# One written-out order for the middle stage of the first sequence, some of its units filtered on GpSimd, and the imaginary filter pieces loaded first

## The chip, the cores and the metric

The kernel runs on one core of a Trainium2 chip. Its time is the device time of one execution in microseconds. Three runs of the kernel before gave 859.03, 859.19 and 859.25 us, a median of 859.19 us. The five engines of the core have one instruction queue each, worked strictly in the order written: TensorE (PE; its weight loads are shown as PEld), VectorE (DVE), ScalarE (ACT), GpSimd (POOL) and SyncE (SP, which here only issues DMAs). An engine at whose head an instruction waits for a semaphore does nothing else meanwhile.

## The reference

The kernel computes a spectral filter along the sequence followed by a normalized gated feed-forward block. It takes x (8 sequences, 3008 positions, 256 channels), a complex filter per frequency and channel (1505 x 256, real and imaginary parts apart), and the weights of the block.

```python
X = np.fft.rfft(x, axis=1)
Y = X * (filt_r + 1j * filt_i)[None, :, :]
x = np.fft.irfft(Y, n=3008, axis=1).reshape(24064, 256)
xn = x / np.sqrt(np.mean(x * x, axis=-1, keepdims=True) + 1e-06) * rms_g
g = xn @ w_gate                                   # 256 -> 1536
out = (g / (1 + np.exp(-g)) * (xn @ w_val)) @ w_out   # 1536 -> 256
```

All matrix products run on fp16 operands with fp32 sums; inputs and output are float32.

## The kernel before

**The transform.** 3008 is 47 x 64. A sequence goes through four matrix stages. Stage A (`a0_unit`, `a_unit`) is a real transform over 64 points, a product with the 128 x 128 table `wa`. Stage B (`b_unit`) is, for each of K2 = 32 values k2, a complex transform over 47 points with twiddle factors, a product of a 96-row tile with the 96 x 96 table `wb[:, k2]`. Then comes the filter. The inverse of B (`bi_unit`, table `wi`) writes the buffer `uu`, and the inverse of A (`n_unit`, table `wai`) gives the filtered sequence. `wb` and `wi` have 128 rows; only the first 96 (KR) enter a product.

**Units.** Stage B, the filter and the inverse of B work in 16 units per sequence, called u = 2 g + dh: g is a group of four k2 and dh one half of the 256 channels. For a unit, four matmuls fill a PSUM tile of 128 x 384 (`psb`). The complex multiplication is two elementwise products, the halves of `s_part`: e = 0 multiplies by the real filter (columns 96 to 143 of `ff`), e = 1 multiplies the tile with real and imaginary parts exchanged by minus the imaginary filter and the imaginary filter (columns 0 to 95 of `ff`). Each half is one VectorE instruction of 128 x 384 (lines 238 and 241).

**Sequence 0 and the others.** Sequence 0 goes ahead of everything and is kept on the chip: between A and B it is turned by TensorE (`tr0_unit`, eight units of four k2, copied from PSUM to the tiles `t2`), and behind the filter `yt0_unit` adds the two halves and turns them in one go, by eight matmuls with the identity into a PSUM tile `psy`, copied to `yt`. Then `bi_unit` follows and its copy into `uu`. The stage from `tr0_unit` to the last copy into `uu` is called the middle stage here. Sequences 1 to 7 are spread over the feed-forward work of the sequence before; they go through memory between A and B (`z_store`, `t2_load`), add their halves on GpSimd and turn by a DMA transpose. For sequence 1, units 2, 6, 10 and 14 already go through `b_soft`: ScalarE copies `psb` to SBUF and GpSimd does both halves (GpSimd does not read PSUM in this kernel).

**The filter.** `f_load(i, f)` loads filter rows in three blocks i of 512 rows, f = 0 the imaginary and f = 1 the real part, into three float32 buffers `fs`. `f_unit(i, f, dh)` turns one block and channel half by four TensorE transposes and copies the pieces into `ff`. `f_neg` then fills the negated imaginary columns on GpSimd, and `f_last` a corner.

**The queue of GpSimd** issues most loads: x (`x_load`), the filter, `wb`, `wi`, the gate and value weights (`w_load`, three thirds q into staging buffers) and the down weights (`wo_load`). The DMAs that GpSimd issues take eight landing semaphores in turn, and an issue waits until the DMA that had its semaphore before has landed. `w_gain(q)` scales a third of the gate and value weights by the norm's gain into `wg` and `wv`. A staging buffer comes free for a new load when what was in it has been read; the four of them serve `fs`, `ws` and later the tiles y.

**Behind the middle stage.** `t4_load` turns `uu` by four DMA transposes on SP's queue. `t4_first` and `first_norm` bring the first tile of 512 positions to the feed-forward block without waiting for these. A small copy `seen` (line 681) holds GpSimd's queue until the second of the four transposes has landed. Then the feed-forward block begins: 8 x 6 tiles of 12 steps each (`gv`: two matmuls for the gate, two for the value, SiLU on ScalarE, product on VectorE; `down`: four matmuls). The work of later sequences is laid between these steps by a plan that is made when the kernel is built (`fit`, `at`): each step has room for one more PSUM tile and some time on ScalarE and VectorE. For sequence 1 the plan puts the 12 `a_unit`s (line 204) one to a step from the fifth on; units 6 to 8 read the x chunk that `x_load(1, 2)` brings, units 9 to 11 that of `x_load(1, 3)`.

**The order around the change** is written out by hand in the block under `tc.manual_schedule()`: first the loads, then `fill`s (matmuls without use for their result), stage A of sequence 0, the filter units between the turning units, and a loop over positions p that runs `b_unit`, both halves, `yt0_unit` two positions later and `bi_unit` four positions later. In it VectorE does all 32 halves, ScalarE nearly all copies of `psy` and `psi`; GpSimd issues loads and runs `f_neg` and all three `w_gain`.

Of the kernel before, what the change touches and what calls it, by code (L numbers as in the profile page):

```python
# [10 lines left out]
FP32 = mybir.dt.float32  # L11
FP16 = mybir.dt.float16
# [8 lines left out]
P = 128  # L21
# [80 lines left out]
def kernel(  # L102
# [83 lines left out]
            nc.gpsimd.dma_start(t.rearrange("p a d -> p (a d)"), src(N2, XC))  # L186
        st[b]["x"][c] = t

    def bank(i, name):
        pool, tag = ((psM, "mx"), (psG, "pg"), (psV, "pv"), (psB, "mb"), (psO, "po0"))[i]  # L190
        return pool.tile([P, 512], FP32, tag=tag, name=name)

    def copy(eng, out, in_, scale=None):
        if eng == "A":
            nc.scalar.activation(out=out, in_=in_, func=AXT.Copy, **({} if scale is None else {"scale": scale}))  # L195
        elif scale is None:
            nc.vector.tensor_copy(out=out, in_=in_)
        else:
            nc.vector.tensor_scalar(out=out, in0=in_, scalar1=scale, scalar2=None, op0=ALU.mult)
# [30 lines left out]
    def s_part(b, i, e, eng=None):  # L230
        eng = eng or nc.vector
        g, dh = divmod(i, 2)
        ps, s = st[b]["s"][i]
        fv = ff[:, dh, 4 * g:4 * g + 4, :]
        o = s[e].rearrange("p k (r q) -> p k r q", r=2)
        if e == 0:
            f1 = fv[:, :, 2 * SL:3 * SL].unsqueeze(2).to_broadcast([P, 4, 2, SL])
            eng.tensor_tensor(out=o, in0=ps, in1=f1, op=ALU.mult)  # L238
        else:
            f2 = fv[:, :, 0:2 * SL].rearrange("p k (r q) -> p k r q", r=2)  # L240
            eng.tensor_tensor(out=o, in0=ps[:, :, ::-1, :], in1=f2, op=ALU.mult)  # L241
# [35 lines left out]
    def yt_tile(b, g):  # L277
        st[b]["yt"][g] = ytp.tile([P, 4, 2, P], FP16, tag="yt", name="yt")
# [90 lines left out]
        copy(eng, va[:, dh].rearrange("p k (m i) -> p (k m) i", m=NR)[:, :, 4 * gq:4 * gq + 4],  # L369
             ps.rearrange("p (u t) -> p t u", u=4))  # L370

    def tr0_unit(g, eng):
        pool, tag = ((psO, "po0"), (psO, "po1"), (psM, "mx"))[g % 3]
        ps = pool.tile([KR, 4, 2, P], FP16, tag=tag, name="pst")
        for k in range(4):
            for dh in range(2):
                nc.tensor.transpose(ps[:, k, dh, :], va[:, dh, 4 * g + k, :], ident)  # L377
        c, r = divmod(g, 2)
        if c not in st[0]["t2"]:
            t2_tile(0, c)  # L380
        copy(eng, st[0]["t2"][c][:, 4 * r:4 * r + 4, :].rearrange("p k (e d) -> p k e d", e=2), ps)
# [13 lines left out]
    def f_unit(i, f, dh, e):  # L395
        t = fst[i]
        ps = bank(1 + "AV".index(e), "psf").rearrange("p (a q) -> p a q", a=FR4)
        for a in range(FR4):
            nc.tensor.transpose(ps[:, a, :], t[:, f, a, ds(dh * P, P)], idf)  # L399
        v = ps.rearrange("p a (q s) -> p s a q", s=16)  # L400
        fk = ff[:, dh, 0:K2].rearrange("p (t k) c -> p t k c", k=4)
        fu = ff[:, dh, 1:K2 + 1].rearrange("p (t k) c -> p t k c", k=4)[:, ::-1, ::-1, :]
        lo = SL * (1 + f) + 8 * i
        hi = lo + H
        if i < 2:
            copy(e, fk[:, :, :, lo:lo + 8], v[:, 0:8])
            copy(e, fu[:, :, :, hi:hi + 8], v[:, 8:16])
        else:
            copy(e, fk[:, :, :, lo:lo + 8], v[:, 8:16])
            copy(e, fu[:, :, :, hi:hi + 7], v[:, 0:8, :, 1:8])  # L410
# [6 lines left out]
    def f_neg(k0, n, dhs=(0, 1)):  # L417
        for dh in dhs:
            nc.gpsimd.tensor_scalar(out=ff[:, dh, k0:k0 + n, 0:SL], in0=ff[:, dh, k0:k0 + n, SL:2 * SL],  # L419
                                    scalar1=-1.0, scalar2=1.0, op0=ALU.mult, op1=ALU.mult)  # L420

    def yt0_unit(i, eng, bk, ks=slice(0, 4)):
        g, dh = divmod(i, 2)
        s = st[0]["s"][i][1]
        ps = bank(bk, "psy")[0:KR].rearrange("p (k t) -> p k t", k=4)
        for k in range(4)[ks]:
            for e in range(2):
                nc.tensor.matmul(ps[:, k, :], s[e][:, k, :], ident, start=(e == 0), stop=(e == 1))  # L428
        if g not in st[0]["yt"]:
            yt_tile(0, g)  # L430
        copy(eng, st[0]["yt"][g][0:KR, ks, dh, :], ps[:, ks])

    def fill(n, bk=0):
        ps = bank(bk, "pf")
# [120 lines left out]

    wst = {}

    def w_load(q):
        cols = ts(q, DFF // 3)
        t = stg.tile([P, 2, 2, DFF // 3], FP32, tag="stg", name="ws")  # L560
        for src, k in ((moe_w_gate, 0), (moe_w_val, 1)):
            nc.gpsimd.dma_start(t[:, k], src.rearrange("(dt p) j -> p dt j", p=P)[:, :, cols])
        wst[q] = t

    def wo_load(q):
        nc.gpsimd.dma_start(wo[:, ts(q, JT // 3), :],
                            moe_w_out.rearrange("(jt p) d -> p jt d", p=P)[:, ts(q, JT // 3), :])
# [10 lines left out]
    with tc.manual_schedule():  # L578
# [19 lines left out]
        nc.vector.memset(mhalf, -0.5)  # L598
        nc.vector.memset(ones, 1.0)
        for t in ss3[1:]:  # L600
# [23 lines left out]
        a0(3)  # L624
        fill(4)
        a0(4, 5)
        todo = [(i, f, dh) for i in range(2) for f in range(2) for dh in range(2)][:7] + [(2, 0, 0)]
        for u in todo[0:2]:
            f_unit(*u, "A")
        for g in range(7):  # L630
            tr0_unit(g, "V")
            if g < 6:
                f_unit(*todo[g + 2], "A")
        f_neg(4, 4, (0,))
        f_neg(8, 8, (0,))
        UN = K2 // 2
        od = [2, 4, 6, 3, 5, 7, 0, 1] + list(range(8, UN))
        tr0_unit(7, "V")
        for p in range(2):
            b_unit(0, od[p], (0, 3)[p], 1)  # L640
        f_unit(1, 1, 1, "A")
        f_unit(2, 0, 1, "A")
        b_unit(0, od[2], 4, 1)
        f_unit(2, 1, 0, "A")
        for p in range(3):
            s_part(0, od[p], 0)
        for p in range(UN + 3):
            if 3 <= p < UN:
                b_unit(0, od[p], (0, 3)[p % 2])
                s_part(0, od[p], 1)  # L650
            if p == 0:
                f_unit(2, 1, 1, "A")
                f_neg(4, 12, (1,))
                f_last()
                f_neg(0, 4)
# [10 lines left out]
            if p == UN + 1:  # L666
                yt0_unit(UN - 1, "V", 1, slice(0, 2))
                yt0_unit(UN - 1, "A", 0, slice(2, 4))
            if 4 <= p < UN + 3:
                bi_unit(0, od[p - 4], "AV"[p == UN + 1], 2)  # L670
            if UN + 1 <= p < UN + 3:
                fill(1, 1)
        bi_unit(0, UN - 1, "V", 3, slice(0, 2))
        bi_unit(0, UN - 1, "A", 0, slice(2, 4))
        a_unit(1, 0, "A", 1)
        t4_first()
        a_unit(1, 1, "V", 0)
# [1 line left out]
        for c in range(NXC):  # L679
            t4_load(0, c)  # L680
        nc.gpsimd.tensor_copy(out=seen, in_=st[0]["t4"][1][:, 0, 0:4])
# [188 lines left out]
```

## Time and profile before

| what | value |
|---|---|
| median of 3 runs | 859.19 us (859.03 to 859.25) |
| profiled execution, device time | 859.02 us |
| its span in the profile | 857.2 us |
| busy, TensorE / VectorE / ScalarE / GpSimd | 849.3 / 556.1 / 612.8 / 300.4 us |
| first filter half on VectorE | 21.54 us |
| last copy into `uu` on VectorE ends | 38.91 us |
| first gate matmul | 43.12 us |
| granted TensorE clock | 1.00 |

Times are counted from the start of the span. The profiled execution takes 1.8 us more than its span, for what lies around it. In the order of time a row gives the start, the length from the first to the last instruction of the row, the engine, the line of the kernel, the operation, the tiles (output <- input) with their sizes, how many instructions are merged in the row, and in brackets how long the engine stood idle before it and what ended the wait. In the table by stretches the columns are the stretch and its length, the busy time and count of instructions of TensorE, weight loads, VectorE, ScalarE and GpSimd, the granted clock, the share of time that the 16 DMA engines were busy, and GB/s. A row on DMA issues gives the size of one and the microseconds from issue to landing.

### The profile page before, as it was taken

The page shows a single profiled execution, that of the slowest core. Times are in us where ns is not written, and L with a number is a line of the kernel's source. Part 1 is how long each engine was busy: PE and PEld are TensorE (multiplying, and loading weights), DVE is VectorE, ACT ScalarE, POOL GpSimd, SP SyncE. Part 2 cuts the span into 40 slices and gives each one's busy share as a digit, 9 for nine tenths or more (in the row PEclk, how much of TensorE's full clock was granted, in tenths as well). Part 3 has the DMA queues.
Part 4 walks back from the last instruction along what each step waited for, and adds up shares of the span by engine and source line. Part 5 has one row for each costly group of instructions (what it writes and reads, how often), then busy time and mean ns, then how long its engine had stood idle before and what let it go on. Part 6 is the DMA issues. An engine that isn't in the chain of part 4 may idle for free.

```text
span 857.2 us, 16980 instructions
## 1 busy us (share of the span) xinstructions
PE 849.3 (99%) x6117; PEld 531.9 (62%) x6117; DVE 556.1 (65%) x922; ACT 612.8 (71%) x1343; POOL 300.4 (35%) x349
## 2 busy tenths in 40 slices
PE   8999999999999999999999999999999999999997
PEld 6756666666656666666666666666666666665654
DVE  5857655776666666666666676767666665555554
ACT  4986878786687757887578865887567765777444
POOL 5725732543154413443144430444123430132000
PEclk9999999999999999999999999999999999999999
DMA  9997698756976566747746648534554331521101
GB/s 284 271 182 151 148 191 162 148 124 143 186 137 133 117 134 119 158 113 129 157 126 110 130 99 172 119 77 117 129 115 93 99 72 41 125 52 50 63 25 50
DMA packets 199293, 108.24 MB, mean 126 GB/s; under 512 B 159622, under 2 KB 183576, under 8 KB 199208
## 3 DMA queue, kind: packets, MB, share of 16 engines
q1 hardware_dynamic: 190520, 85.78, 44.2%
q0 software_dynamic: 8544, 21.24, 12.8%
q8 instruction: 48, 0.79, 0.4%
q14 instruction: 37, 0.30, 0.1%
q10 hardware_dynamic: 144, 0.13, 0.0%
HBM read 45.78 MB, written 35.65 MB: 95 GB/s over the span
## 4 chain that ended last, share of the span: by engine, by line
PE 97%; DMA 1%; DVE 0%; ACT 0%; POOL 0%; issue 0%; POOLq 0%
PE po L526 29%; PE pv L501 28%; PE pg L501 28%; PE psb L248 3%; PE psi L292 3%; PE psn L321 2%; PE psa L204 2%; DMA fs<-in_filt_i_dram 1%; PE psy L428 1%; PE psf L399 1%; PE pst L377 0%; POOL xc L186 0%; DVE s L238 0%; ACT ff L195 0%; ACT sq L458 0%
## 5 line engine op out<-in xcount | busy, mean ns | idle before, releaser
L506 DVE TENSOR_TENSOR hh<-pv,sg 128x512 f16<-128x512 f32 (+1 forms) x577 | 391.5, 679 | 284.0 <-ACT sg L505 219.9
L505 ACT ACTIVATE sg<-pg 128x512 f16<-128x512 f32 (+1 forms) x577 | 337.5, 585 | 214.5 <-PE pg L501 210.7
L501 PE MATMUL pg<-xn,wg 128*128 128x512 f16 (+2 forms) x1156 | 337.9, 374 | 0.0
L501 PE MATMUL pv<-xn,wv 128*128 128x512 f16 (+2 forms) x1156 | 337.8, 374 | 0.0
L526 PE MATMUL po<-wo,hh 128*128 128x256 f16 x2256 | 332.6, 272 | 0.0
L526 PEld LDWEIGHTS <-hh 128*128 128x128 f16 x2256 | 213.5, 98 | 105.5
L275 POOL TENSOR_TENSOR ss<-s,s 128x384 f16<-128x384 f16 x112 | 101.9, 911 | 267.1 <-DVE s L241 239.5
L501 PEld LDWEIGHTS <-wv 128*128 128x128 f16 x1156 | 113.0, 98 | 130.6 <-issue 0.2
L501 PEld LDWEIGHTS <-wg 128*128 128x128 f16 x1156 | 111.6, 98 | 16.8 <-issue 0.2
L347 POOL TENSOR_TENSOR xt<-y,rho 128x1024 f16<-128x1024 f32 (+1 forms) x47 | 87.3, 1858 | 2.9
L329 ACT ACTIVATE junk<-y 128x256 f16<-128x256 f32 x184 | 76.0, 413 | 2.9
L241 DVE TENSOR_TENSOR s<-psb,ff 128x384 f16<-128x384 f32 x124 | 67.6, 547 | 0.3 <-POOL ff L419 0.3
L238 DVE TENSOR_TENSOR s<-psb,ff 128x384 f16<-128x384 f32 x124 | 67.6, 547 | 0.3 <-ACT ff L195 0.2
L195 ACT ACTIVATE uu<-psi 128x384 f16<-128x384 f32 (+1 forms) x127 | 61.8, 487 | 1.0
L195 ACT ACTIVATE y<-psn 128x512 f32<-128x512 f32 (+1 forms) x95 | 55.8, 588 | 4.4 <-PE psn L321 0.2
L292 PEld LDWEIGHTS <-yt 96*128 96x128 f16 x512 | 35.5, 97 | 26.2 <-issue 0.2
L339 POOL TENSOR_TENSOR rho<-u,mhalf 128x4 f32<-128x4 f32 (+1 forms) x47 | 47.6, 1012 | 3.9
L337 POOL TENSOR_SCALAR u<-ss 128x4 f32<-128x4 f32 (+1 forms) x47 | 9.1, 194 | 106.4 <-ACT junk L329 105.2
L292 PE MATMUL psi<-wi,yt 96*128 96x96 f16 x512 | 42.9, 205 | 0.0
L195 ACT ACTIVATE t<-psa 128x512 f16<-128x512 f32 x69 | 40.9, 594 | 2.4 <-PE psa L204 0.9
L248 PE MATMUL psb<-wb,t 96*128 96x96 f16 x480 | 40.0, 206 | 0.0
L248 PEld LDWEIGHTS <-t 96*128 96x128 f16 x480 | 29.3, 97 | 10.7 <-issue 0.2
(91 smaller groups left out, 361.0 us busy)
## 6 DMA issues: line engine op xcount, KB each, us to landing
out_dram<-o SPq DMA_DIRECT2D x40, 512.0 KB, 3.6
xc<-in_x_dram POOLq DMA_DIRECT2D x31, 384.0 KB, 5.7
z_tmp<-t SPq DMA_DIRECT2D x28, 384.0 KB, 2.6
t<-z_tmp SPq DMA_DIRECT2D x28, 384.0 KB, 6.0
out_dram<-o SPq DMA_DIRECT2D x7, 384.0 KB, 3.1
fs<-in_filt_i_dram POOLq DMA_DIRECT2D x3, 512.0 KB, 10.7
fs<-in_filt_r_dram POOLq DMA_DIRECT2D x3, 512.0 KB, 11.3
ws<-in_moe_w_gate_dram POOLq DMA_DIRECT2D x3, 512.0 KB, 10.0
```

Of the source, the lines that this page charges most:

```text
L195: nc.scalar.activation(out=out, in_=in_, func=AXT.Copy, **({} if scale is None else {"scale": scale}))
L238: eng.tensor_tensor(out=o, in0=ps, in1=f1, op=ALU.mult)
L241: eng.tensor_tensor(out=o, in0=ps[:, :, ::-1, :], in1=f2, op=ALU.mult)
L248: nc.tensor.matmul(ps[:, ts(k, KR)], st[b]["t2"][kk // KC][:, kk % KC, ds(dh * P, P)], wb[0:KR, kk, :], start=True, stop=True)
L275: nc.gpsimd.tensor_tensor(out=ss3[g % 3][:, :, dh, 0:KR], in0=s[0], in1=s[1], op=ALU.add)
L292: nc.tensor.matmul(ps[:, k, :], yt[0:KR, k, dh, :], wi[0:KR, 4 * g + k, :], start=True, stop=True)
L329: nc.scalar.activation(out=junk, in_=y[:, i, ts(u, D)], func=AXT.Square, accum_out=ss[:, 2 * i + u:2 * i + u + 1])
L347: nc.gpsimd.tensor_tensor(out=xt[:, 0:n, :], in0=y.rearrange("p a (u d) -> p (a u) d", u=2)[:, 0:n, :], in1=rho[:, 0:n].unsqueeze(2).to_br ...
L501: nc.tensor.matmul(ps[:, (r0 - q0) * P:(r1 - q0) * P], wt[:, dt_, ts(jt, P)], xn[:, r0:r1, dt_, :], start=(dt_ == 0), stop=(dt_ == 1))
L505: nc.scalar.activation(out=sg[:, c], in_=pg[:, 0:w], func=AXT.Silu)
L506: nc.vector.tensor_tensor(out=hh[:, c], in0=pv[:, 0:w], in1=sg[:, c], op=ALU.mult)
L526: nc.tensor.matmul(po[q - 1][:, 0, :] if own else po[q // 2][:, q % 2, :], hh_of[(b, m, j)][:, ts(q, P)], wo[:, j, :], start=(j == 0 and ( ...
```

## The change

The first half of the diff concerns helpers; the second replaces the loop of the middle stage by a string of steps.

- The loads of the filter are issued as three imaginary blocks, a piece of `wb`, three real blocks. `wb` and `wi` are loaded with 96 rows. The thirds 1 and 2 of the gate and value weights are issued on SP's queue; they stood on GpSimd's.
- The middle stage is a string, read from left to right. A token is a step, a unit (hexadecimal), an engine for the copy where there is one (A ScalarE, V VectorE) and a PSUM bank: T turning unit, F filter unit (block, part, channel half), N `f_neg` (channel half, range of k2), B stage B, S one half of the filter on VectorE, P both halves on GpSimd after a copy by ScalarE (`s0_soft`), Y adding and turning, I inverse of B, L `f_last`, D a load (`x_load(1,0)`, `wo_load(0)`, `x_load(1,1)`). The tokens of each engine keep this order in its queue.
- Four tokens P stand in the string: units e, 9, 0 and d. The other 12 units are filtered on VectorE. Three of the turned tiles (a, f, d) and four of the inverse copies into `uu` (9, 3, f, 1) are copied by VectorE; of the turning units 0, 3, 4, 6 and 7 by VectorE, 1, 2 and 5 by ScalarE; three filter units by VectorE.
- The halves are kept in five pairs of buffers that go round as they come free, one of them in the tile `tail`; the turned tiles in eight slots.
- `w_gain(0)`, `w_gain(1)`, `wo_load(1)` and the copy `left` stand behind the string; `x_load(1, 2)` stands behind `seen`, ahead of `wo_load(2)` and `x_load(1, 3)`, and `w_gain(2)` behind those.

```diff
-    def tr0_unit(g, eng):
-        pool, tag = ((psO, "po0"), (psO, "po1"), (psM, "mx"))[g % 3]
-        ps = pool.tile([KR, 4, 2, P], FP16, tag=tag, name="pst")
+    def tr0_unit(g, eng, bk):
+        ps = bank(bk, "pst", [KR, 4, 2, P], FP16)
...
+    def s0_soft(u):
+        s0_get(u)
+        ps, s = st[0]["s"][u]
+        v = xnp.tile([P, 4, 2, P], FP16, tag="xn", name="v").rearrange("p a b c -> p (a b c)").bitcast(FP32)
+        v = v[:, 0:4 * KR].rearrange("p (k r q) -> p k r q", k=4, r=2)
+        nc.scalar.activation(out=v, in_=ps, func=AXT.Copy)
+        st[0]["s"][u] = (v, s)
+        for e in range(2):
+            s_part(0, u, e, nc.gpsimd)
...
-    def w_load(q):
+    def w_load(q, eng):
...
-            nc.gpsimd.dma_start(t[:, k], src.rearrange("(dt p) j -> p dt j", p=P)[:, :, cols])
+            eng.dma_start(t[:, k], src.rearrange("(dt p) j -> p dt j", p=P)[:, :, cols])
...
-        for n in range(6):
-            if n == 5:
-                nc.gpsimd.dma_start(wb[:, 4:16, :], wb_d[:, 4:16, :])
-            f_load(*divmod(n, 2))
-        nc.gpsimd.dma_start(wb[:, 16:K2, :], wb_d[:, 16:K2, :])
-        nc.gpsimd.dma_start(wb[:, 0:4, :], wb_d[:, 0:4, :])
-        nc.gpsimd.dma_start(wi, wi_d)
-        w_load(0)
-        w_load(1)
+        for i in range(3):
+            f_load(i, 0)
+        nc.gpsimd.dma_start(wb[0:KR, 4:16, :], wb_d[0:KR, 4:16, :])
+        for i in range(3):
+            f_load(i, 1)
+        nc.gpsimd.dma_start(wb[0:KR, 16:K2, :], wb_d[0:KR, 16:K2, :])
+        nc.gpsimd.dma_start(wb[0:KR, 0:4, :], wb_d[0:KR, 0:4, :])
+        nc.gpsimd.dma_start(wi[0:KR], wi_d[0:KR])
+        w_load(0, nc.gpsimd)
+        w_load(1, nc.sync)
+        w_load(2, nc.sync)
...
+        order = """
+            T3V4 T1A1 F001V3 D0 T7V2 T2A4 F100V2 F101A1 F000A2 T5A0 T4V4 F200V2 D1 D2 N01 F201A1 T6V3 F010A1
+            N02 B24 F111A5 N12 B42 S21 N11 F110A0 B63 F210A1 N13 S41 S61 B55 S51 F011A1 F211A0 S60 Be2 N03
+            S40 S20 L T0V1 Pe Y6A1 Y4A2 Y2A3 Bb4 N00 Ba1 B90 S50 Sb0 P9 N10 I6A2 Sb1 Y5A5 Sa0 Sa1 B72 I2A1
+            YbA0 YeA4 S70 I5A1 Bc5 S71 Sc0 YaV3 B32 B00 P0 I4A4 Y7A1 Y9A1 Sc1 S31 S30 Bd3 IeA4 Bf2 Pd YcA5
+            Sf1 B81 IbA0 S80 Y3A1 B12 Y0A3 S81 I7A5 Sf0 IcA4 S11 S10 IaA1 I9V0 YfV2 Y8A1 YdV3 Y1A2 I3V1 I0A4
+            IfV5 I8A2 IdA3 I1V2
+        """
...
+        loads = ((x_load, 1, 0), (wo_load, 0), (x_load, 1, 1))
...
-            if p == 0:
-                f_unit(2, 1, 1, "A")
-                f_neg(4, 12, (1,))
...
-                w_load(2)
-                wo_load(0)
-                f_neg(16, 16)
-                wo_load(1)
-                for c in range(3):
-                    x_load(1, c)
-                for q in range(3):
-                    w_gain(q)
-            if 2 <= p < UN + 1:
-                yt0_unit(od[p - 2], "A", 1)
...
+        w_gain(0)
+        w_gain(1)
+        wo_load(1)
+        nc.gpsimd.tensor_copy(out=left, in_=uu[:, H - 1, :, :].rearrange("p e (k m) -> p e k m", k=K2)[:, :, :, 0:2])
         a_unit(1, 0, "A", 1)
         t4_first()
...
         nc.gpsimd.tensor_copy(out=seen, in_=st[0]["t4"][1][:, 0, 0:4])
+        x_load(1, 2)
         wo_load(2)
         x_load(1, 3)
+        w_gain(2)
         first_norm()
```

More of the change, by code (lines that the diff above doesn't have):

```diff
@@ L425, in yt0_unit @@
         ps = bank(bk, "psy")[0:KR].rearrange("p (k t) -> p k t", k=4)
-        for k in range(4)[ks]:
+        for k in range(4):
             for e in range(2):
                 nc.tensor.matmul(ps[:, k, :], s[e][:, k, :], ident, start=(e == 0), stop=(e == 1))
-        if g not in st[0]["yt"]:
-            yt_tile(0, g)
-        copy(eng, st[0]["yt"][g][0:KR, ks, dh, :], ps[:, ks])
+        n = len(y0)
+        if n < 8 and n % 2 == 0:
+            t = ytp.tile([P, 4, 2, P], FP16, tag="yt", name="yt").rearrange("p a b c -> p (a b c)")
+            y0_slots.extend(t[0:KR, ts(h, 512)].rearrange("p (k t) -> p k t", k=4) for h in range(2))
@@ L433, in fill, with bi0_unit @@
+        y0[u] = y0_slots[n % 8]
+        copy(eng, y0[u], ps)
+    def bi0_unit(u, eng, bk):
+        g, dh = divmod(u, 2)
+        ps = bank(bk, "psi")[:, 0:4 * KR].rearrange("p (k j) -> p k j", k=4)
+        for k in range(4):
+            nc.tensor.matmul(ps[:, k, :], y0[u][:, k, :], wi[0:KR, 4 * g + k, :], start=True, stop=True)
+        copy(eng, uu[:, :, dh, 16 * g:16 * g + 16].rearrange("p c (k m) -> p c k m", k=4),
+             ps.rearrange("p k (c m) -> p c k m", c=H))
     def fill(n, bk=0):
@@ L626 @@
         a0(4, 5)
[L627 to L640, printed above, removed]
@@ new lines @@
+        """
+        for i in range(4):
+            s0_free.append([sp.tile([P, 4, KR], FP16, tag="s%d" % e, name="s%d" % e) for e in range(2)])
+        v = tail.rearrange("p q d -> p (q d)").bitcast(FP16)
+        s0_free.append([v[:, ts(e, 4 * KR)].rearrange("p (k q) -> p k q", k=4) for e in range(2)])
+        loads = ((x_load, 1, 0), (wo_load, 0), (x_load, 1, 1))
+        for w in order.split():
+            k, n = w[0], int(w[1:2] or "0", 16)
+            if k == "T":
+                tr0_unit(n, w[2], int(w[3]))
+            elif k == "F":
+                f_unit(n, int(w[2]), int(w[3]), w[4], int(w[5]))
+            elif k == "N":
+                f_neg(*((0, 4), (4, 4), (8, 8), (16, 16))[int(w[2])], (n,))
+            elif k == "L":
+                f_last()
+            elif k == "B":
+                b0_unit(n, int(w[2]))
+            elif k == "S":
+                s0_get(n)
+                s_part(0, n, int(w[2]))
+            elif k == "P":
+                s0_soft(n)
+            elif k == "D":
+                loads[n][0](*loads[n][1:])
+            else:
+                (yt0_unit if k == "Y" else bi0_unit)(n, w[2], int(w[3]))
```

48 lines of the change are left out of this document (20 added, 28 removed).

## The prediction

> **What bounds the kernel now.** I read the page's table of busy times and its slices, then the chain of work that ended last, then the busy times in stretches of 10 us, then the order of time of each engine up to 60 us.
>
> ```profile
> span 857.2 us, 16980 instructions
> PE 849.3 (99%) x6117; PEld 531.9 (62%) x6117; DVE 556.1 (65%) x922; ACT 612.8 (71%) x1343; POOL 300.4 (35%) x349
> PE 97%; DMA 1%; DVE 0%; ACT 0%; POOL 0%; issue 0%; POOLq 0%
> ```
>
> TensorE is the path for nearly the whole span. From 50 us up to the end of the last tile it has no idle time, so a microsecond is won only ahead of the first gate matmul (43.12 us), and a microsecond of TensorE waiting behind that point is lost one for one.
>
> ```profile
> 10.00:20.00 10.00, 9.37 (x121) 8.57 (x119) 6.16 (x10) 6.69 (x19) 4.33 (x7) 1.00 1.03 397
> 20.00:30.00 10.00, 9.07 (x144) 8.09 (x142) 9.42 (x20) 7.82 (x21) 8.62 (x16) 1.00 1.02 390
> 30.00:40.00 10.00, 9.86 (x154) 7.98 (x153) 8.77 (x20) 9.62 (x23) 9.33 (x15) 1.00 1.06 194
> 50.00:60.00 10.00, 10.00 (x61) 5.76 (x60) 5.38 (x9) 8.31 (x18) 3.97 (x5) 1.00 0.88 206
> ```
>
> The columns are TensorE, weight loads, VectorE, ScalarE, GpSimd, granted clock, DMA share, GB/s. To 30 us DMA is full; in the middle stage VectorE and ScalarE run one behind the other, so TensorE's "busy" there is waiting strung between short matmuls. Now the marks in time, VectorE first, then GpSimd, then TensorE:
>
> ```profile
> 21.54 1.50 DVE L241 TENSOR_TENSOR s<-psb,ff 128x384 f16<-128x384 f32 x3 [0.32 <-POOL ff L419]
> 23.25 2.10 DVE L238 TENSOR_TENSOR s<-psb,ff 128x384 f16<-128x384 f32 x4 [0.21 <-ACT ff L195]
> 36.42 0.54 DVE L241 TENSOR_TENSOR s<-psb,ff 128x384 f16<-128x384 f32 x1
> 38.55 0.36 DVE L197 CAST uu<-psi 128x192 f16<-128x192 f32 x1 [0.17 <-PE psi L292]
> ...
> 20.30 0.72 POOL L562 DMA_DIRECT2D ws<-in_moe_w_val_dram  x1 [1.06 <-DMA wb<-wb_t]
> 21.14 0.84 POOL L419 TENSOR_SCALAR ff<-ff 128x192 f32<-128x192 f32 x2
> 45.89 0.19 POOL L681 COPY seen<-t 128x4 f16<-128x4 f16 x1 [6.56 <-DMA t<-uu]
> 46.02 0.81 POOL L566 DMA_DIRECT2D wo<-in_moe_w_out_dram  x1
> 46.82 0.61 POOL L186 DMA_DIRECT2D xc<-in_x_dram  x1
> ...
> 51.98 0.38 PE L204 MATMUL psa<-xc,tab 128*128 128x512 f16 x1
> 56.53 0.38 PE L204 MATMUL psa<-xc,tab 128*128 128x512 f16 x1
> ```
>
> The stage is VectorE's queue of filter halves, from 21.54 (first imaginary half) and 23.25 (first real half) to the last inverse copy, done at 38.91. GpSimd shows the trap: a DMA issue holds its queue until an older load has landed (20.30, for `wb`), and the first negated filter piece stands behind it.
>
> **The change part by part.**
>
> *Load order.* The last filter piece lands at 10.03 + 11.3 = 21.3. Ahead of it stand the same pieces; only the `wb` piece is 96 rows of 128, 74 KB less, at the 0.41 MB/us of these stretches 0.18 us: 21.1. Between the second imaginary piece's neighbour at 18.0 (6.18 + 11.8) and `wb` at 20.0 (8.11 + 11.9) only 288 KB lie, some 0.7 us of transfer: one engine lags, and the one instruction-fetch packet in 16 to 18 us (3.4% of 16 engines over 2 us, 1.09 us of one engine) is what I find for it. If that falls behind the last piece, it lands at 20.0. I take 21.1, as before; ends 20.0 and 21.3.
>
> *The wait it adds.* D0, D1, D2 (`x_load`, `wo_load`, `x_load`) now stand on GpSimd ahead of all `f_neg`. There are eight landing lanes in turn, and D2 takes the lane of the last real filter piece. So N01, the first negation, waits for all six filter pieces, although it reads imaginary ones only. By the row of before (landed 20.0, issue 20.30, negation 21.14, done about 21.50) N01 starts 1.14 us after 21.1 and S21, the first filter half, 0.40 later: 22.6, against 21.54. Loading the imaginary pieces first gives VectorE nothing while D2 stands there.
>
> *VectorE's queue.* The order string holds four P (e, 9, 0, d), not five: 12 units stay, 24 halves at a start-to-start of 0.47 (28 steps from 23.25 to 36.42), 11.3 us. Added: T0 at 0.59 (two such copies take 1.28), Ya 0.60. Behind the last half: four inverse copies at 0.46 and two Y at 0.60, 3.0. Sum 15.5: 22.6 + 15.5 = 38.1, with hand-overs and the last copy's end 38.3. Before it ended at 38.91: 0.6 us won. With the ends of the landing: 0.4 to 1.7.
>
> *ScalarE.* The first Y needs S60 and S61, so about 25.7. From there 13 Y at 0.50, 12 I at 0.38, three v copies at 0.38 (the 384-wide copy row): 12.2, to 37.9, just under VectorE. TensorE, from 25.1: 16 x 0.45 + 16 x 0.18 + 11 x 0.18 = 12.1, to 37.2. Neither is the bound.
>
> *GpSimd.* Six negations, about 3.0, from 22.2; f_last 0.5; two negations 0.5; eight soft halves at 0.96 (rows of 990 to 1000 ns in sequence 1), 7.7; about 0.9 of waits for v: the last soft half ends near 34.8, Yd needs it at 35.5. It hides, with 0.7 to spare. Two `w_gain`, 8 x 0.67 = 5.4, end at 40.2; the gate matmul needs the first at 42.5. The third, behind `seen` and three issues, ends near 51; column block 8 needs it at 54.15 less the shift. Hidden. The normalization of tile 1 (50.90 to 54.2) slips by up to 1 us, and its transposed tile, landed by 57.33, is read at 61.7: hidden.
>
> *Weights on SP.* 2 MB move to SP's queue, waiting for the filter buffers' last transposes (about 22). They can delay `wi`, landed at 24.5 before; the first I needs it at 26.9. I put nothing; if it lost half the rate, 25.3, still nothing.
>
> *x(1,2), x(1,3) and wo.* This is what I charge. x(1,2) was issued by 31 us. Now it stands behind `seen`, with `wo_load(2)` and x(1,3) behind it, and `wo_load(1)` moves from 28.49 to about 40.5, into the four DMA transposes. In the clock of before x(1,2) is needed at 51.98 and x(1,3) at 56.53.
>
> ```profile
> wo<-in_moe_w_out_dram POOLq DMA_DIRECT2D x1, 256.0 KB, 5.9
> xc<-in_x_dram POOLq DMA_DIRECT2D x1, 384.0 KB, 8.1
> ```
>
> These two, issued at 46.02 and 46.82, landed at 51.9 and 54.9; the second had 1.6 us to spare. From 46 to 48.5 only the hardware queue (the transposes) moved anything. In 48.5 to 51 the small `wo` rows took the engines. An x load more takes 2.0 (393 KB at the 0.2 MB/us of 60.5 to 61.5) to 2.7 us (the x load from 59.0 to 61.75). So x(1,3) lands 2.0 to 2.7 later, plus what of `wo_load(1)`'s 2.6 us does not fit the idle DMA gap at 43 to 44, 0 to 1.6: 56.9 to 59.2, that is 0.4 to 2.7 us late. x(1,2) itself, first in line, lands at 51.2 to 53.5; its wait is the earlier part of the same one and is not added. I take 1.3, nearer the low end, since part of `wo_load(1)` fits. TensorE has no idle time there to give it back.
>
> **Sum.** 857.2 span, 859.02 with what lies around it: 859.02 - 0.6 + 1.3 = 859.7. The median of the runs, 859.19, is 0.17 above the profiled execution: 859.9.
>
> **Rivals.** (1) *The stage gains its full end and the loads are in time.* The fetch lag falls behind the filters (20.0), and x(1,3) finds the engines free as the lone 4.5 us issue-to-landing row of x(2,0) has it: -1.7, 857.5. For it: DMA is drained by 39 us. Against: the transposes held the software queue out for 2.5 us.
>
> (2) *The late x loads decide* (other side). x(1,3) lands at 59.2, 2.7 late, and the stage wins 0.4: +2.3, 861.5. It is over 0.2% from a lateness of 2.3 us on. For it: nothing moved on the software queue in 46 to 48.5, so `wo_load(1)` would stand in front of x(1,2) at 48.5. Against: the gap at 43 to 44.
>
> (3) *The clock drops.* The first ten fills take 4.45 us, 0.445 each; the four at 10.26, later on, take 1.03 in all. In the new order TensorE idles about 1.5 us (23.6 to 25.1) where it idled 0.79, after which its eight transposes still took 0.45. Were the clock halved for 3.4 us there, with TensorE needed some nine tenths of the time, it costs about 1.7: 861.6. [...]
>
> (4) *The change does not do what it says.* Four units, not five, filter on GpSimd. A fifth would take 0.94 from VectorE and put 1.9 on GpSimd, where only 0.7 is spare; my sum is for four.
>
> **How the numbers follow.** Forecast (859.9; its own range 858.4 to 860.9): 0.55. Rival 1: 0.15. Rival 2: 0.23. Rival 3: 0.04. The rest, 0.03, is an unseen wait. A bound of 0.2% is 1.72 us, 857.47 to 860.91. Rival 1 sits on its line and gives most of 0.13 faster; rivals 2, 3 and the rest give 0.29 slower; 0.58 is left within. Range 857.6 to 861.7: rivals 1 and 2 to their prices.
>
> **What would show it.** Right: S21 near 22.6, just behind D2 and N01 on GpSimd; the last uu copy near 38.3; TensorE waiting for an x load ahead of the seventh or tenth `psa` of sequence 1. Wrong: filter halves before 21.5 (D2 does not hold), the last uu copy before 37 or after 39, or no TensorE idle time between 50 and 60 us. If GpSimd's soft halves take over 1.1 us each, Yd becomes the end of the stage.

## The result, and the profile after

The changed kernel takes 864.0 us (median of four runs, 863.07 to 865.07), against 859.19 before: ratio 1.0057, with a 95% interval of 1.0039 to 1.0074. It is slower by 4.8 us. The prediction said 859.9, with a range of 857.6 to 861.7, and was wrong. The profiled execution took 863.56 us with a span of 861.8, 4.6 us more than the span before, and all of these 4.6 us can be found in the trace ahead of 57 us.

The page of the changed kernel, its first line and its chain of work that ended last:

```profile
span 861.8 us, 16974 instructions
PE 94%; DMA 4%; issue 0%; POOL 0%; ACT 0%; DVE 0%; DVEq 0%; SPq 0%; POOLq 0%
```

DMA's share of the chain rose from 1% to 4%, TensorE's fell from 97% to 94%: TensorE now waits for data at places where it did not. The stretch from 20 to 24 us of the kernel before, and then two stretches of this kernel, in the columns of the prediction (TensorE, weight loads, VectorE, ScalarE, GpSimd, granted clock, DMA share, GB/s):

```profile
20.00:24.00 4.00, 3.08 (x37) 2.57 (x35) 3.47 (x7) 2.48 (x9) 2.64 (x7) 1.00 1.02 397
...
20.00:24.00 4.00, 2.98 (x35) 2.68 (x33) 0.34 (x1) 2.58 (x8) 1.55 (x3) 1.00 1.00 241
50.00:60.00 10.00, 7.93 (x48) 4.45 (x47) 3.36 (x5) 6.81 (x17) 7.77 (x11) 1.00 1.10 201
```

Two things stand out. From 20 to 24 us VectorE worked for 0.34 us, and DMA, though its share is still 1.00, moved 241 GB/s where the kernel before moved 397. And from 50 to 60 us TensorE lost two microseconds where it had been busy without a break. In the order of time, VectorE, then GpSimd, then TensorE (its last row, set apart, is the second `psn` of the kernel before):

```profile
24.20 1.96 DVE L241 TENSOR_TENSOR s<-psb,ff 128x384 f16<-128x384 f32 x4 [3.86 <-POOL ff L418]
38.22 1.59 DVE L197 CAST uu<-psi 128x384 f16<-128x384 f32 x3
```

```profile
23.11 0.57 POOL L186 DMA_DIRECT2D xc<-in_x_dram  x1 [1.62 <-DMA fs<-in_filt_r_dram]
23.77 3.22 POOL L418 TENSOR_SCALAR ff<-ff 128x192 f32<-128x192 f32 x6
41.86 0.83 POOL L601 DMA_DIRECT2D wo<-in_moe_w_out_dram  x1
49.82 0.19 POOL L712 COPY seen<-t 128x4 f16<-128x4 f16 x1 [6.82 <-DMA t<-uu]
50.05 0.57 POOL L186 DMA_DIRECT2D xc<-in_x_dram  x1
```

```profile
44.09 0.38 PE L536 MATMUL pg<-xn,wg 128*128 128x256 f16 x2
49.81 0.39 PE L321 MATMUL psn<-t,tab 128*128 128x512 f16 x1 [1.24 <-DMA t<-uu]
56.60 0.39 PE L204 MATMUL psa<-xc,tab 128*128 128x512 f16 x1 [2.07 <-DMA xc<-in_x_dram]
...
47.43 0.38 PE L321 MATMUL psn<-t,tab 128*128 128x512 f16 x1
```

The loss has three parts.

- *The middle stage*: the first gate matmul starts at 44.09 us, 43.12 before: +0.97, where 0.6 were to be won. VectorE idled 3.86 us ahead of its first filter half, for the negated filter pieces of GpSimd, which stood behind D2, which waited for the last real filter piece. That piece landed at 22.5 (issued at 10.22, 12.3 us to landing), 21.3 before.
- *The second `psn` of the first transposed tile* waits 1.24 us for a DMA transpose of `uu`. Counted from the first gate matmul, it starts 1.41 later than before (49.81 - 44.09 against 47.43 - 43.12).
- *The seventh `psa` of sequence 1* waits 2.07 us for x(1,2). Before, it ran 8.86 us behind the first gate matmul (51.98 - 43.12), now 12.51: 3.65 more, of which 1.41 are the `psn` and 2.24 its own.

0.97 + 1.41 + 2.24 = 4.62, the difference of the spans. The tenth `psa`, which needs x(1,3), doesn't wait.

### The profile page after: what moved, and what is told of

It is laid out like the page before. It is cut to its first block, busy times and chain, and to the rows that moved or that the text cites. A ratio compares the mean times of both kernels' runs of the same rounds, so it can differ in the third digit from the quotient of the medians.

```text
span 861.8 us, 16974 instructions
## 1 busy us (share of the span) xinstructions
PE 846.9 (98%) x6115; PEld 530.7 (62%) x6115; DVE 554.6 (64%) x921; ACT 612.1 (71%) x1338; POOL 304.9 (35%) x354
## 4 chain that ended last, share of the span: by engine, by line
PE 94%; DMA 4%; issue 0%; POOL 0%; ACT 0%; DVE 0%; DVEq 0%; SPq 0%; POOLq 0%
PE po L561 28%; PE pv L536 28%; PE pg L536 28%; PE psn L321 2%; PE psi L292 2%; PE psb L248 2%; PE psa L204 2%; DMA xc<-in_x_dram 2%; DMA fs<-in_filt_r_dram 1%; DMA t<-uu 1%; PE psy L452 1%; PE psi L464 0%; PE psb L432 0%; POOL xc L186 0%; ACT uu L195 0%
## 5 line engine op out<-in xcount | busy, mean ns | idle before, releaser
L241 DVE TENSOR_TENSOR s<-psb,ff 128x384 f16<-128x384 f32 x120 | 65.3, 547 | 3.9 <-POOL ff L418 3.9
L238 DVE TENSOR_TENSOR s<-psb,ff 128x384 f16<-128x384 f32 x120 | 65.3, 547 | 0.0
L195 ACT ACTIVATE uu<-psi 128x384 f16<-128x384 f32 x124 | 60.4, 492 | 0.9
L292 PEld LDWEIGHTS <-yt 96*128 96x128 f16 x448 | 31.6, 97 | 25.9
L292 PE MATMUL psi<-wi,yt 96*128 96x96 f16 x448 | 37.5, 205 | 0.0
L321 PE MATMUL psn<-t,tab 128*128 128x512 f16 x94 | 35.2, 375 | 1.2 <-DMA t<-uu 1.2
L248 PE MATMUL psb<-wb,t 96*128 96x96 f16 x432 | 36.1, 206 | 0.0
```

The source lines that it names most:

```text
L292: nc.tensor.matmul(ps[:, k, :], yt[0:KR, k, dh, :], wi[0:KR, 4 * g + k, :], start=True, stop=True)
```

## Experiments

Each kernel below starts from the changed kernel, unless another is named; kernel 6 is that of experiment 6, and so on. All times are medians; the ratio is against the kernel before, run beside them.

**1. Are the loads of 96 rows slow?** Load order and row count changed together, and the real filter pieces landed late, so one of them had to be separated.

```diff
-        nc.gpsimd.dma_start(wb[0:KR, 4:16, :], wb_d[0:KR, 4:16, :])
+        nc.gpsimd.dma_start(wb[:, 4:16, :], wb_d[:, 4:16, :])
...
-        nc.gpsimd.dma_start(wi[0:KR], wi_d[0:KR])
+        nc.gpsimd.dma_start(wi, wi_d)
```

> The changed kernel with wb and wi loaded with 128 rows again, nothing else. Theory (the 96-row pieces slow the DMA engines while they move, and so push the last real filter piece from 21.3 us to 22.5): the last piece lands near 21.3, the first filter half starts near 23.0 instead of 24.20, the first gate matmul comes near 42.9 instead of 44.09, and the time falls by about 1.2 us to 862.8; both waits of TensorE behind the first gate matmul (1.2 and 2.1 us) stay. Rival (the new order of the filter pieces, or the x load D0 issued among them, makes the last piece late): first half within 0.3 us of 24.20, time within 0.4 us of 864.

862.68 us (861.92 to 864.03), ratio 1.0043 [1.0028, 1.0058]. The stretch from 20 to 24 us and the first filter half of this kernel:

```profile
20.00:24.00 4.00, 3.68 (x49) 3.44 (x45) 1.45 (x4) 3.88 (x13) 2.89 (x6) 1.00 1.01 394
22.85 1.97 DVE L241 TENSOR_TENSOR s<-psb,ff 128x384 f16<-128x384 f32 x4 [2.56 <-POOL ff L418]
```

More bytes, and yet they are there sooner: 394 GB/s against 241, and `wi` lands 9.8 us behind its issue, where the smaller one of the changed kernel took 12.0. The first half starts 1.35 us earlier than in the changed kernel, the first gate matmul at 42.74, 0.4 before that of the kernel before. So the load order isn't what made the stage lose; the 96 rows are. By the medians the time falls by 1.3 us, as much as the stage. The profiled execution, 864.03 us, is the slowest of the four and doesn't show this gain, because of a thing that I hadn't looked for. TensorE, around its wait for x(1,2), and the stretch behind it:

```profile
55.28 0.61 PE L204 MATMUL psa<-xc,tab 128*128 128x512 f16 x1 [2.31 <-DMA xc<-in_x_dram]
56.53 1.06 PE L536 MATMUL pg<-xn,wg 128*128 128x512 f16 x2
```

```profile
55.30:58.70 3.40, 3.40 (x11) 1.50 (x12) 0.14 (x1) 1.19 (x2) 1.22 (x1) 0.50 1.17 186
```

The granted clock is 0.50 for 3.4 us behind that wait, and two gate matmuls take 1.06 us in place of 0.59. The mean granted clock of this execution is 0.997; the other three, of 861.92 to 862.93 us, have 0.999 or 1.00. The last experiment returns to this.

**2. Does D2 hold the negations?** The lines are pieces of the order string.

```diff
-  T4V4 F200V2 D1 D2 N01 F201A1
+  T4V4 F200V2 N01 F201A1
...
-  S60 Be2 N03
+  S60 Be2 N03 D1 D2
```

> The changed kernel with the tokens D1 and D2 (wo_load(0) and x_load(1,1)) moved from ahead of the negations to behind the last of them (N03). Theory (the wait of D2 for the last filter piece holds the negations): N01 starts near 20, the first filter half near 20.6 instead of 24.20, the four imaginary halves are done before the last real piece is in, the first real half starts near 24.0 instead of 26.08, the last copy into uu ends 1.5 to 2 us earlier, and the time falls by 1.5 to 2 us. Rival (the two issues only change places with the negations on a GpSimd queue that is full either way, and its late soft halves become the end of the stage): the first filter half is early, but the first gate matmul comes within 0.4 us of 44.09 and the time stays.

864.22 us (862.64 to 864.62), ratio 1.0056 [1.0041, 1.0071]. VectorE and then TensorE in the middle stage of this kernel:

```profile
20.16 0.56 DVE L241 TENSOR_TENSOR s<-psb,ff 128x384 f16<-128x384 f32 x1
...
24.66 0.56 DVE L241 TENSOR_TENSOR s<-psb,ff 128x384 f16<-128x384 f32 x1 [1.90 <-PE psb L432]
...
23.75 0.63 PE L398 MATMUL psf<-tab,fs 128*128 128x128 f32 x4 [1.59 <-DMA fs<-in_filt_r_dram]
```

The hold is real: with the two loads gone from in front, the first half starts at 20.16, 4.04 us sooner. But it brings little. The fourth half waits for `psb` of B55, and B55 stands in TensorE's queue behind F210, which waits until 23.75 for the last real piece (13.6 us from issue to landing here, 12.3 in the changed kernel; why isn't settled); the first real half starts at 25.14. The first gate matmul comes at 43.55, 0.54 sooner. The profiled execution (864.62 us) again has 3.4 us of clock 0.50 behind a wait of 2.27 us for x(1,2), which takes the gain away; two of the others have the same low mean clock, 0.997, and the one with 0.999 took 862.64 us. An early VectorE is worth little while TensorE's order ties it to the same landing.

**3. Is x(1,2) late because of where it is issued?**

```diff
+        x_load(1, 2)
         w_gain(0)
...
-        x_load(1, 2)
         wo_load(2)
```

> The changed kernel with x_load(1,2) issued ahead of w_gain(0) instead of behind the copy seen. Theory (two causes behind the first gate matmul, one after the other): the wait of 2.07 us ahead of the seventh psa of sequence 1 is gone, the wait of 1.24 us ahead of the second psn stays or grows by some tenths, and the time falls by 1.8 to 2.2 us. Rival (one cause: all that is late there is late because the transposes are, and the next read behind them waits instead): the wait moves to the tenth psa, which reads x(1,3), and the time falls by less than 0.7 us.

860.67 us (859.72 to 861.33), ratio 1.0016 [1.0007, 1.0026]: 3.3 us less than the changed kernel. In the profiled execution the first gate matmul comes at 43.93, nearly unmoved, and both waits are gone, the one for x(1,2) and the one for the transpose. The second was not expected to go. This execution is the fastest of the ten, 0.95 us under the median, so the others may still have waited; no trace shows it. GpSimd in this kernel:

```profile
36.35 0.64 POOL L186 DMA_DIRECT2D xc<-in_x_dram  x1
42.34 0.81 POOL L601 DMA_DIRECT2D wo<-in_moe_w_out_dram  x1
47.78 0.19 POOL L713 COPY seen<-t 128x4 f16<-128x4 f16 x1 [4.32 <-DMA t<-uu]
```

The early load pushes `wo_load(1)` from 41.86 to 42.34, and here its packets moved only from 46 us on, behind most of the transposes. In the changed kernel they moved from 44 us on, among them: from 44 to 45 us the software queue moved 0.06 MB and the transposes 0.07, where in the next experiment's kernel the transposes, alone, moved 0.21 MB in the same microsecond.

**4. Does `wo_load(1)` slow the transposes, and through them `seen` and x(1,2)?**

```diff
+        wo_load(1)
         w_gain(0)
         w_gain(1)
-        wo_load(1)
```

> The changed kernel with wo_load(1) issued ahead of w_gain(0) instead of behind w_gain(1), so that its rows are in before the four transposes begin. Theory (its 512-byte rows share the engines with the transposes, the second transpose lands late, and the copy seen holds x_load(1,2) for as long): the wait of 1.24 us ahead of the second psn is gone, seen comes about 2.9 us after the first gate matmul instead of 5.7, the wait for x(1,2) shrinks from 2.07 to about 0.6, and the time falls by about 3 us. Rival 1 (two causes that do not hang together): the wait for psn goes and the one for x(1,2) stays near 2.1; the time falls by 1.2. Rival 2 (the transposes stop for another reason, such as the instruction fetch that stands among them): both waits stay and so does the time.

861.61 us (861.01 to 862.65), ratio 1.0030 [1.0020, 1.0040]. GpSimd and TensorE in this kernel:

```profile
47.83 0.19 POOL L712 COPY seen<-t 128x4 f16<-128x4 f16 x1 [4.25 <-DMA t<-uu]
...
55.08 0.39 PE L204 MATMUL psa<-xc,tab 128*128 128x512 f16 x1 [1.37 <-DMA xc<-in_x_dram]
```

The first gate matmul comes at 44.68, 0.6 later than in the changed kernel, as the last filter piece landed at 23.1 here. `seen` runs 3.15 us behind it, 5.73 in the changed kernel, 2.77 before, and the four transposes take 8.01 us from first to last, 10.49 in the changed kernel, 8.08 before. The wait of the `psn` is gone and the one for x(1,2) is down to 1.37. So the waits hang together: the `wo` rows slow the transposes, `seen` holds GpSimd, and x(1,2) stands behind `seen`. Even without the first step x(1,2) is late by its place alone, and by more than the 0.6 us expected.

**5. Do 96 rows cost as much in the kernel before?** The kernel before, with only the row count of `wb` and `wi` changed.

```diff
-        nc.gpsimd.dma_start(wb[:, 16:K2, :], wb_d[:, 16:K2, :])
+        nc.gpsimd.dma_start(wb[0:KR, 16:K2, :], wb_d[0:KR, 16:K2, :])
...
```

> The kernel before, with nothing but its wb and wi loads cut to 96 rows; order of the loads as before. Theory (the 96-row pieces are slow for what they carry: 0.48 MB per 2 us in 20 to 24 us against 0.80 in the kernel before): the last real filter piece and the wb pieces land about 1 us later, the first real filter half starts near 24.3 us (23.25 before), the first gate matmul near 44.1 (43.12), and as TensorE has nothing to give back behind it the time rises by about 1.0 to 860.1. Rival (the lateness needs the new load order, in which a 96-row piece stands ahead of three real blocks; here only one block stands behind it): first gate matmul within 0.3 us of 43.12 and the time within 0.4 of 859.1.

859.51 us (859.05 to 860.78), ratio 1.0005 [0.9996, 1.0015]. DMA slows in the same way, and the first real half is later, though by 0.6 us only:

```profile
20.00:24.00 4.00, 3.00 (x38) 2.63 (x35) 2.81 (x6) 2.29 (x10) 2.01 (x5) 1.00 1.01 262
23.86 2.10 DVE L238 TENSOR_TENSOR s<-psb,ff 128x384 f16<-128x384 f32 x4 [1.07 <-ACT ff L195]
```

The last real piece landed at 22.4 (10.21 + 12.2), 1.1 us later than before, as the theory said; the first gate matmul came at 43.72, 0.6 later. The profiled execution is 0.7 us longer than that of the kernel before; the median rose by 0.3 us, which the interval doesn't tell from nothing. Neither number of the expectation was met. In the old order VectorE had three imaginary halves to do and 1.9 us between the landing and its first real half, and that takes up half of the delay. In the new order nothing was in between.

**6. Do the row count and the two loads explain the whole loss?**

```diff
-        nc.gpsimd.dma_start(wb[0:KR, 4:16, :], wb_d[0:KR, 4:16, :])
+        nc.gpsimd.dma_start(wb[:, 4:16, :], wb_d[:, 4:16, :])
...
+        x_load(1, 2)
+        wo_load(1)
         w_gain(0)
         w_gain(1)
-        wo_load(1)
...
-        x_load(1, 2)
         wo_load(2)
```

> The changed kernel with two parts put back: wb and wi loaded with 128 rows, and x_load(1,2) and wo_load(1) issued ahead of w_gain(0). Theory (the whole loss is the slow 96-row pieces plus these two late loads): first gate matmul near 42.7 us, as with 128 rows alone, no TensorE wait of over 0.3 us behind it, no window with a granted clock of 0.5, time 859.1 - 0.4 = 858.7. Rival (the transposes and the x loads still meet, because everything behind the string now starts 1.2 us sooner): a wait of 1 us or more at the second psn of tile 1 or at the seventh psa, time 859.7 or more.

858.72 us (858.53 to 859.00), ratio 0.9995 [0.9986, 1.0004]: 5.3 us less than the changed kernel and the 858.7 of the theory. The first gate matmul comes at 43.00, and from 42 to 64 us TensorE waits nowhere for more than 0.2 us:

```profile
50.00:60.00 10.00, 10.00 (x62) 5.79 (x61) 5.38 (x9) 8.31 (x18) 4.30 (x6) 1.00 0.86 200
```

The change's string of steps, taken with old row counts and early loads, is thus worth about half a microsecond by the medians, which the interval doesn't tell from nothing. The prediction had put 0.6 on the stage.

**7. What does the stage give when nothing holds VectorE?** Kernel 6, with the two loads behind N03 as in 2, and one token moved on TensorE.

```diff
-  S21 N11 F110A0 B63 F210A1 N13 S41 S61 B55 S51
+  S21 N11 F110A0 B63 B55 F210A1 N13 S41 S61 S51
```

> The kernel of the run above, and the two loads D1 and D2 moved behind N03, and B55 moved ahead of F210, so that TensorE brings the fourth imaginary product before it waits for the last real filter piece. Theory (the hold of GpSimd by D2 and then TensorE's order kept VectorE from the imaginary halves): first half near 20.2 us, four imaginary halves done by 22.5, first real half near 23, first gate matmul near 41.1, no waits behind it, time 859.1 - 2.0 = 857.1, faster than the kernel before. Rival (once VectorE is early, another engine sets the stage: GpSimd's soft halves, ScalarE's copies or TensorE behind the real filter pieces): first half early all the same, but the first gate matmul within 0.4 us of the run above and the time within 0.4 of it, near 858.7.

857.40 us (857.13 to 857.78), ratio 0.9980 [0.9971, 0.9988]: faster than both kernels, 1.8 us under the one before. The first half, the first real half and the first gate matmul of this kernel:

```profile
20.09 0.56 DVE L241 TENSOR_TENSOR s<-psb,ff 128x384 f16<-128x384 f32 x1
23.17 1.49 DVE L238 TENSOR_TENSOR s<-psb,ff 128x384 f16<-128x384 f32 x3 [0.38 <-ACT ff L195]
...
41.53 0.38 PE L536 MATMUL pg<-xn,wg 128*128 128x256 f16 x2
```

Four imaginary halves now run while the last real piece lands (21.6), is turned and copied. VectorE's queue, which sets the stage in this order, starts earlier, and neither ScalarE nor GpSimd takes its place. The 1.3 us from kernel 6 are what the hold and TensorE's order cost together; taken alone, in experiment 2, taking the hold away moved the first gate matmul by 0.54.

**8. What is filtering on GpSimd worth?** Kernel 7, with the four units on VectorE.

```diff
-  T0V1 Pe Y6A1    B90 S50 Sb0 P9 N10    B00 P0 I4A4    Bf2 Pd YcA5
+  T0V1 Se0 Se1 Y6A1    B90 S50 Sb0 S90 S91 N10    B00 S00 S01 I4A4    Bf2 Sd0 Sd1 YcA5
```

> The kernel of the run above with its four P tokens replaced by pairs of S, so that VectorE does all 32 halves of sequence 0 and ScalarE makes no copy for GpSimd. It measures what filtering four units on GpSimd is worth. Theory (VectorE's queue is the stage): eight halves more at 0.47 us are 3.8 us, less little for the copies that ScalarE saves; first gate matmul 2.5 to 3.8 us later than in the run above, time 2.5 to 3.8 us longer. Rival (the stage is set by ScalarE or by the landing of filters and wi, and VectorE has room): first gate matmul and time within 0.7 us of the run above.

860.36 us (860.23 to 860.59), ratio 1.0013 [1.0004, 1.0022]: 2.96 us more than kernel 7, with the first gate matmul at 44.52, 2.99 later. The four P are worth 3.0 us, of the 3.8 (8 x 0.47) that they take from VectorE's queue; what gives back the other 0.8 wasn't looked for. From 30 to 40 us VectorE of this kernel has no idle time, and GpSimd works for 2.7 us only:

```profile
30.00:40.00 10.00, 8.63 (x154) 7.70 (x151) 10.00 (x22) 7.78 (x18) 2.72 (x4) 1.00 1.08 250
```

**9. Is it 96 that is slow, or all that isn't 128?** `wb` and `wi` with 112 rows:

```diff
-        nc.gpsimd.dma_start(wb[0:KR, 16:K2, :], wb_d[0:KR, 16:K2, :])
+        nc.gpsimd.dma_start(wb[0:112, 16:K2, :], wb_d[0:112, 16:K2, :])
...
```

> The changed kernel with wb and wi loaded with 112 rows, in place of 96. Theory (the loads go slower the further they are from 128 rows): 300 to 350 GB/s in 20 to 24 us, between the 241 of 96 rows and the 394 of 128; first gate matmul between 43.1 and 43.7 us; time 863.2 to 863.8. Rival (only a load over all 128 rows goes fast): 250 GB/s or less in 20 to 24 us, first gate matmul at 44.1 or later, time 864.0 or more.

865.45 us (864.57 to 866.26), ratio 1.0073 [1.0058, 1.0088]. The rival is the nearer of the two: 267 GB/s from 20 to 24 us, a little above its bound of 250 but far from the 300 to 350 of the theory, and the first gate matmul at 44.66, 0.6 later still than with 96 rows. That more bytes go at nearly the same low rate would explain this, but one execution doesn't prove it: with 96 rows the last piece landed as late or later in experiments 2 and 4. In the profiled execution (mean clock 0.997) the clock fell as in experiment 1, two gate matmuls taking 1.06 us behind a wait of 2.32, and one more has a mean clock of 0.998; the other two have 0.999 and 1.00 and took 865.22 and 864.57 us.

```profile
20.00:24.00 4.00, 2.34 (x29) 2.05 (x26) 0.25 (x1) 2.02 (x7) 1.09 (x2) 1.00 1.04 267
```

**10. Does the wait make the clock fall?** The wait ahead of the seventh `psa` is made longer.

```diff
-        x_load(1, 2)
         wo_load(2)
         x_load(1, 3)
+        x_load(1, 2)
         w_gain(2)
```

> The changed kernel with x_load(1,2) moved behind x_load(1,3), so that TensorE's wait ahead of the seventh psa grows from 2.07 us to about 4.2 (the second of the two x loads landed near 59.0 in the changed kernel, and the matmul's turn is at 54.5). Theory (an idle time of TensorE of over 2 us or so in the feed-forward part makes the granted clock fall to 0.5 for 3.41 us, as in the profiled runs with 128 rows alone and with the loads behind N03): a window of 0.5 in the profiled execution, and a time of 864.0 + 2.3 + 1.7 = 868.0. Rival (the fall in those two runs had nothing to do with the wait): granted clock 1.00 throughout, time 864.0 + 2.3 = 866.3.

869.28 us (869.24 to 870.38), ratio 1.0122 [1.0105, 1.0139]. TensorE in this kernel, and two stretches:

```profile
60.07 0.61 PE L204 MATMUL psa<-xc,tab 128*128 128x512 f16 x1 [5.95 <-DMA xc<-in_x_dram]
```

```profile
54.10:57.60 3.50, 0.03 (x1) 0.00 (x0) 0.69 (x1) 0.23 (x1) 3.25 (x4) 1.00 1.17 223
57.60:64.40 6.80, 4.33 (x15) 2.18 (x16) 0.69 (x1) 1.79 (x3) 0.92 (x3) 0.52 0.78 156
```

The wait grew to 5.95 us, by 3.88 rather than 2.1. The clock is full for the first 3.8 us of it and at half for the next 6.8. In the profiled executions, the longer wait and the first gate matmul (43.66, 0.43 sooner) would give 863.56 + 3.88 - 0.43 = 867.0; it was 869.31, so 2.3 us are left for the clock. By estimate that is what it costs: from 60.07 to 64.8 TensorE works at half the clock, and these 4.7 us hold work for half as long. All four executions have a mean clock of 0.995 or 0.996. The theory holds; its 1.7 was for one such period, and here there were two.

## Why the prediction was wrong, step by step

- *Load order*: this term failed. I let the 96-row `wb` piece land by its bytes, 0.18 us earlier, and put the last piece at 21.1 with ends at 20.0 and 21.3. It landed at 22.5. Experiments 1, 5 and 9 show why: with loads of 96 or 112 rows under way DMA moved 225 to 267 GB/s in the traces in place of 394 to 398. The bound was drawn from rows that were all of 128-row loads, so no end of it covered this.
- *The wait it adds*: right. D2 held the negations until all six pieces had landed. From the real landing my step gives 22.5 + 1.14 + 0.40 = 24.0 for the first half; it was 24.20. Experiment 2 shows the hold by its absence. What I didn't see is that TensorE's queue held the fourth imaginary half by the same landing.
- *VectorE's queue*: right. 15.5 us were worked out from first half to last copy; the last copy ended at 39.81, 15.6 behind 24.20. The stage came out at +0.97 against -0.6 because its first half started 1.6 us later than I put it, and 1.4 of these are the landing.
- *ScalarE, GpSimd and the weights on SP*: right as far as the runs tell. `wi` landed at 26.6 (14.61 + 12.0), later than the 25.3 that I took for the worse case, but the first inverse matmul, at 28.60, didn't wait for it. In the changed kernel no copy or half waits for GpSimd behind the negations, and four P are worth 3 us (experiment 8). There were four, as rival 4 of the prediction said; a fifth wasn't tried.
- *x(1,2), x(1,3) and wo*: the term was 1.3 and measured 3.65. The place was right, the chain was wrong. I charged `wo_load(1)` only as bytes ahead of x(1,3) and said that the wait for x(1,2) wasn't to be added. In fact its rows ran among the four transposes, which took 10.49 us on SP's queue from first to last instead of 8.08; the `psn` waited for one of them (1.41), `seen` ran at 49.82 instead of 45.89, x(1,2) was issued behind it at 50.05 and landed 6.5 later. What decided was x(1,2), and x(1,3) had no wait of its own. Rival 2 named the right sort of loss, on the other load, and put it at 2.7 us against the 3.65.
- *Rival 3, the clock*: it doesn't fall in the middle stage, where I put it; in the changed kernel's profiled execution it doesn't fall in mid-work at all (1.00). Its price assumed half the clock for 3.4 us, which no row of the kernel before shows (1.00). Experiments 1, 2, 9 and 10 show it, 0.50 for 3.4 us and twice as long in 10, behind the late x load.
- *Rival 1*, a stage that wins its full end and loads in time, has the number of kernel 7 (857.5 against 857.40), but that is luck. It was to come from a last filter piece landing at 20.0; in kernel 7 that piece landed at 21.6, and the gain came from imaginary halves that were done before its filter was turned and copied (23.17). It took four repairs that the change lacked (128 rows, x(1,2) and `wo_load(1)` early, D1 and D2 behind the negations, B55 ahead of F210).

## What to carry to other kernels

A transfer that carries fewer bytes can take longer: these loads, issued by GpSimd, were fastest at the full 128 rows (394 to 398 GB/s from 20 to 24 us, against 225 to 267 with 96 or 112), so try a trimmed load on its own and look at the GB/s of the stretch. When a step is moved behind a copy that waits for a DMA, follow what shares the DMA engines with the transfer waited for, and add the waits along that chain rather than the bytes alone: here four transposes took 10.49 us with the `wo` rows among them and 8.01 without (experiment 4). An engine freed early gains little while the engine that feeds it waits, in its own order, for the same transfer: in experiment 2 a first half 4.04 us sooner brought 0.54 at the first gate matmul.

## What the runs showed of the hardware that was not expected

**Rows and rate.** With every load over 128 rows DMA moved 394 to 398 GB/s from 20 to 24 us (five traces), and the last filter piece landed at 21.3 to 21.6; with `wb` and `wi` over 96 rows it moved 225 to 262 (six traces), over 112 rows 267 (one), with the DMA engines as busy (a share of 1.00 to 1.04, against 1.01 to 1.02), and the piece landed at 22.1 to 23.6. What makes the rate fall with the rows isn't shown by any run.

**The clock.** In mid-work the granted clock fell to 0.50 for 3.4 us in four profiled executions, behind waits of TensorE of 2.31, 2.27, 2.32 and, for two such periods, 5.95 us; it didn't fall behind the 2.07 us of the changed kernel or the 1.37 of experiment 4, nor where there was no such wait (the kernel before and experiments 3, 5, 6, 7 and 8). In experiment 1 the low period begins within 0.1 us of the end of the wait (55.28 us); in the 3.4 us ahead of it TensorE had been busy for about 1.1. In experiment 2 it begins some 1.1 us behind the end of the wait, in experiment 10 some 2.1 us ahead of it; by what rule the clock falls isn't shown. The mean clock of the other executions is on record too; one fall takes 0.002 off it by estimate (half of 3.4 us in 862). In experiments 1, 2 and 9 those with 0.997 or 0.998 (one, three and two of four) took longer than all those with 0.999 or 1.00, so the same kernel falls in one execution and not in another. How long the executions without a profile waited isn't known.

**Spread.** The times of experiments 6, 7 and 8, with 128 rows and no late load, lie within 0.4 to 0.65 us. With 96 rows they spread over 1.6 to 1.7 us (3 and 5), with 128 rows and the late load over 2.1 (1), half of it by the one execution in which the clock fell. But the kernel before, with 128 rows, spread over 1.2 us in its 33 executions, so that the slow loads make the time less certain is likely and not shown.

**A standstill of DMA.** Soon after the feed-forward part begins, DMA moved almost nothing for about a microsecond in three kernels: 4 GB/s from 43 to 44 us in the kernel before, 7 GB/s from 44 to 45 in kernel 6, 27 GB/s from 46 to 47 in the changed kernel. In the changed kernel and in kernel 6 a packet of the instruction queue falls in the two microseconds ahead of it, the only one between 42 and 49 us. The four transposes that the next tile needs are under way then, so half a microsecond in the start of `wo_load(1)` (experiment 3) may well decide whether its rows run ahead of the standstill or behind it, and whether a matmul waits. What causes the standstill wasn't tried.
